# Where the layer steps sit among the attention slots, and two shared score tiles in one stretch

## The chip, the core and the metric

The kernel runs on one core of a Trainium2 chip. A core has a matrix engine (TensorE, PE in the profile, with its weight loads listed apart as PEld), a vector engine (VectorE, DVE), an activation engine (ScalarE, ACT), a general engine (GpSimd, POOL) and DMA queues that move data; here SyncE (SP) issues the transfers. Each engine works through its own list of instructions in the order in which the program was written, and waits at an instruction until what it needs has been signalled by another engine. The metric is the device time of one execution in microseconds. The kernel before took 533.57 us (median of 3 runs, 533.13 to 533.61); the profiled execution spans 532.0 us.

## What is computed

Two stages. The first is attention with a threshold: scores that are more than `tau` below the largest of their row are dropped. The second is two matrix layers with `h - tanh(h)` between them, on the 4608 rows that attention gives.

```python
# q, k, v: (8 batches, 8 heads, 576 rows, 64);  tau = 0.02
def _attn_ref(q, k, v, tau):
    scale = 1.0 / np.sqrt(q.shape[-1])
    scores = scale * np.matmul(q, k.transpose(0, 1, 3, 2))
    thresh = np.max(scores, axis=-1, keepdims=True) - tau
    scores = np.where(scores >= thresh, scores, -1000000000.0)
    scores = scores - np.max(scores, axis=-1, keepdims=True)
    attn = np.exp(scores)
    attn = attn / (np.sum(attn, axis=-1, keepdims=True) + 1e-09)
    return np.matmul(attn, v)

# x: (4608, 512), w_in: (512, 2048), w_out: (2048, 512)
def _moe_ref(x, w_in, w_out):
    h = x @ w_in
    g = h - np.tanh(h)
    return g @ w_out
```

## The kernel before

**Pairs and tiles.** The 64 heads are worked in 32 pairs of heads, 4 pairs to a batch. A pair has 9 score tiles of 128 query rows by 576 keys: four for each head, and one that is shared, in which 64 rows belong to one head and 64 to the other (576 is four times 128 and 64 over). In even pairs the shared tile is the last of the nine, in odd pairs the first, so that the shared tiles of pairs 0 and 1, 2 and 3, and so on are neighbours.

```python
TPP = 9                      # tiles of a pair
HPAIR = H // 2               # 4 pairs of a batch
NTILE = NPAIR * TPP          # 288 tiles
AHEAD, MASK, LAG = 8, 5, 2

def kind(i):
    return "AB"[i % 2]

def place(i):
    p, j = divmod(i, TPP)
    j = j - p % 2
    return (p, None, 4) if j in (-1, 8) else (p, j // 4, j % 4)
```

**Scores.** TensorE makes a tile in one of two PSUM buffers, and VectorE scales it into SBUF and takes the row maximum on the way (L341 in the profile). A normal tile is four matmuls with a 128x128 stationary operand. A shared tile is eight with a 128x64 one, which go in twos, one to each half of the output rows (L322).

```python
ps_big = pool("ps_big", 2, space=PSUM)
sc_pool = pool("sc", AHEAD - MASK + 2)
def scores(i):
    p, hh, t = place(i)
    ...
    ps = ps_big.tile([P, 1024], F32, name="psS", tag="big")
    ...
    if hh is None:
        ...
        for n, kk in enumerate((kT, kS)):
            for dst, srcs in ((main, MAIN), (rem, REM)):
                for hh in range(2):
                    nc.tensor.matmul(                              # L322
                        out=ps[64 * hh : 64 * hh + 64, dst],
                        lhsT=qT[:, qrem[hh]], rhs=kk[:, srcs[hh]],
                        start=(n == 0), stop=(n == 1),
                    )
    else:
        ...                                                        # L331, 128x128
    sc = sc_pool.tile([P, S], F32, name="sc")
    ...
    nc.vector.tensor_scalar(                                       # L341
        out=sc, in0=ps[:, lo : lo + S], scalar1=SC, scalar2=None,
        op0=ALU.mult, op1=ALU.max, accum_out=mx[:, c : c + 1],
    )
```

`shift` turns the maxima of a tile A and the B after it into one bias `nb` (DVE, L353). `kink` applies the threshold on ScalarE (L368, writes `z`). Two `z` tiles are transposed by one DMA (`zT`), from pair 6 on, and exponentiated by one ScalarE instruction (`pT`, L404); in the first six pairs TensorE transposes them. `attend` multiplies by `v` (L425 and L432 for a normal tile, L443 for a shared one), `norm` divides, `emit_x` brings the result into the layout of the layers (`xT`).

**The turn of a pair.** Some slots before a pair's first tile, TensorE transposes its `k` with nine 128x128 matmuls (L240) into a PSUM buffer of the same two as the scores; VectorE copies that out as `kT` (L263), and GpSimd makes `kS`, the same with its halves exchanged (L269). `q` is transposed in the same way or, from pair 8 on in three pairs of four, by DMA.

**The layers.** A batch is 512 rows in one layer stage of its own; the 64 rows that each batch leaves over make a ninth stage. A stage has 16 `h` steps (four 512-column matmuls L498, a tanh on ScalarE L511, and the subtraction on VectorE L517) and 16 `y` steps (four 512-column matmuls L524; after four of them a copy and a store). `layers(stage)` lists them: 19 entries for stage 0, and 32 for each of stages 1 to 6, `h` and `y` by turns.

**The slots.** The program is written slot by slot, one score tile to a slot, and in each slot every engine's list gets the pieces that are due. A batch has 36 slots. The layer steps of a batch are woven into the slots of the next one.

```python
for s in range(-AHEAD, NTILE + LAG + 3):
    p, j = divmod(max(s, 0), TPP)
    if 0 <= s < NTILE and j == 2 + LAG and p % HPAIR == 0 and p >= HPAIR:
        assert not todo
        todo = layers(stage, False)
        share = len(todo) / (HPAIR * TPP - 2 - LAG)
        done, stage = 0.0, stage + 1
    if s == NTILE:
        todo = layers(stage, True)
        share, done, stage = 1, 0.0, stage + 1
    if 0 <= s + AHEAD - 1 < NTILE:
        shift(s + AHEAD - 1)
    if 0 <= s + AHEAD < NTILE:
        scores(s + AHEAD)
    ...
    for i in kinks.pop(s, []):
        kink(i)
    bend()                        # tanh of the h step of the slot before
    for i in wts.pop(s, []):
        weights(i)
    if 0 <= s < NTILE + FIRST:
        if todo:
            done += share
            if s < NTILE and j == TPP - 1 and p % HPAIR == HPAIR - 1:
                done = 1e9
            while todo and done >= 1:
                todo.pop(0)()     # a layer step
                done -= 1
    ...
    shrink()                      # the subtraction of that h step
    ...                           # stores; attend, norm and emit_x that are due
    for step in plan.pop(s, []):  # loads, splits, turns of pairs to come
        step()
```

A stage starts in slot 4 of a batch (its `xT` is finished in slot 3) and ends with the batch's last slot. The first four slots of a batch hold no layer step. After the last score tile the rest of the layers (stages 7 and 8) runs alone.

Of the kernel before, what the change touches and what calls it, by code (L numbers as in the profile page):

```python
# [18 lines left out]
def kernel(  # L19
# [14 lines left out]
    B, H, S, D = q.shape  # L34
# [11 lines left out]
    HPAIR = H // 2  # L46
    NPAIR = B * HPAIR
# [4 lines left out]
    TPP = 9  # L52
    NTILE = NPAIR * TPP
# [9 lines left out]
    AHEAD = 8  # L63
    LDK = 16
    MASK = 5
    LAG = 2
# [177 lines left out]
    def q_by_dma(p):  # L244

        return p >= 2 * HPAIR and p % 4 != 0
# [25 lines left out]
    def turn_first(t, part):  # L272

        hl = hls[0, t[0]]
        c0, c1 = ((0, 5), (5, TPP))[part]
        pl, tag = (ps_y, "y") if t == "ks" else (ps_h, "h")
        ps = pl.tile([P, 5 * P], FP16, name=f"ps1_{t}", tag=tag)
        for c in range(c0, c1):
            o = ps[:, (c - c0) * P : (c - c0 + 1) * P]
            if t == "ks":  # L280
                for a in range(2):
                    turn_chunk(o[64 * a : 64 * a + 64, :], c, hl[:, c, 1 - a, :])
            else:
                turn_chunk(o, c, hl[:, c, :, :].rearrange("p a d -> p (a d)"))
        if part == 0:
            mats[0, t] = qk_pool.tile([P, W], FP16, name=f"{t}T", tag=t)
        dst, n = mats[0, t][:, c0 * P : c1 * P], (c1 - c0) * P
        if part == 1 or t == "q":
            nc.scalar.copy(out=dst, in_=ps[:, 0:n])
        else:  # L290
            nc.vector.tensor_copy(out=dst, in_=ps[:, 0:n])
# [6 lines left out]
# [12 lines that stand above are left out]
        qT, kT, kS = mats[p, "q"], mats[p, "k"], mats[p, "ks"]  # L310
        ps = ps_big.tile([P, 1024], F32, name="psS", tag="big")
        main, rem, lo = slice(0, 512), slice(512, 576), 0
        if kind(i) == "B":
            main, rem, lo = slice(512, 1024), slice(448, 512), 448
        if hh is None:
            qrem = REM
            if q_by_dma(p):
                qrem = (slice(512, 640, 2), slice(513, 640, 2))
# [9 lines that stand above are left out]
            lhs = qT[:, (5 * hh + t) * P : (5 * hh + t + 1) * P]  # L328
            for n, kk in enumerate((kT, kS)):
                for dst, src in ((main, MAIN[hh]), (rem, REM[hh])):  # L330
                    nc.tensor.matmul(  # L331
                        out=ps[:, dst], lhsT=lhs, rhs=kk[:, src],
                        start=(n == 0), stop=(n == 1),
                    )
        sc = sc_pool.tile([P, S], F32, name="sc")
        if kind(i) == "B":
            mx = mxs[i] = mxs.pop(i - 1)
        else:
            mx = mxs[i] = mx3[i // 2 % len(mx3)]
        c = int(kind(i) == "B")  # L340
# [4 lines that stand above are left out]
        scs[i] = sc  # L345

    def shift(i):

        if kind(i) == "A":
            return  # L350
        mx = mxs.pop(i)
        nb = st_pool.tile([P, 9], F32, name="nb", tag="nb")
        nc.vector.tensor_scalar(  # L353
            out=nb.rearrange("p (a b) -> p a b", b=3)[:, :, 0:2],
            in0=mx.rearrange("p (a b) -> p a b", b=4)[:, :, 0:3],
            scalar1=-1.0, scalar2=tau, op0=ALU.mult, op1=ALU.add,
        )
        nbs[i - 1], nbs[i] = nb[:, 0:1], nb[:, 1:2]

    def kink(i):  # L360
        sc, nb = scs.pop(i), nbs.pop(i)
        if kind(i) == "B":
            zt = zs.pop(i - 1)
            z = zt[:, S:W]
        else:
            zt = zs[i] = z_pool.tile([P, W], BF16, name="z")
            z = zt[:, 0:S]
        nc.scalar.activation(  # L368
            out=z, in_=sc, func=ACT.Prelu, bias=nb, scale=1.0, alpha=STEEP
        )  # L370
        if on_pe(i):
            zts[i] = zt
        elif kind(i) == "B":
            zts[i] = zt_pool.tile([P, TPP, P], BF16, name="zT")
            nc.sync.dma_start_transpose(out=zts[i], in_=zt)
# [131 lines left out]
    def bend():  # L507
        while halves:
            m, n, ps = halves.pop(0)
            th = t_pool.tile([P, MB], F32, name="th")  # L510
            nc.scalar.activation(out=th, in_=ps, func=ACT.Tanh)  # L511
            ths.append((m, n, ps, th))

    def shrink():
        while ths:
            m, n, ps, th = ths.pop(0)
            nc.vector.scalar_tensor_tensor(  # L517
                out=gs[m][:, n, :], in0=th, scalar=-1.0, in1=ps,
                op0=ALU.mult, op1=ALU.add,
            )  # L520
# [109 lines left out]
    def w_cast():  # L630
        flat, wt, i, cols = loaded.pop(0)
        nc.gpsimd.tensor_copy(out=flat[:, i * cols : (i + 1) * cols], in_=wt)
# [26 lines left out]
    for p in range(1, NPAIR):  # L659
        first = TPP * p - AHEAD  # L660
        for d, f in PREP[3 if p == 1 else 0 :]:
            d -= p == 1 and d in (3, 5)
            if d in (7, 8) and q_by_dma(p):
                d = d + 2
            if p in (2, 4):
                d = {8: 9, 7: 8, 5: 6}.get(d, d)
            elif d == 5 and p >= 5:
                d = 6 if p % 2 else 3
            plan.setdefault(first - d, []).append(lambda p=p, f=f: f(p))
        d = 7 if q_by_dma(p) else 3 - (p == 1 or p >= 5)  # L670
        d = 4 if p in (2, 4) else d
# [16 lines left out]
    todo, stage = [], 0  # L688
# [4 lines left out]
            plan.setdefault(-AHEAD, []).extend(plan.pop(at))  # L693


    kinks, wts, atts = {}, {}, {}
    for i in range(NTILE + 3):
        at = i - 4 if i < HPAIR * TPP else i
# [4 lines left out]
    for s in range(-AHEAD, NTILE + LAG + 3):  # L703
        p, j = divmod(max(s, 0), TPP)
        if 0 <= s < NTILE and j == 2 + LAG and p % HPAIR == 0 and p >= HPAIR:
            assert not todo
            todo = layers(stage, False)
            share = len(todo) / (HPAIR * TPP - 2 - LAG)
            done, stage = 0.0, stage + 1
        if s == NTILE:  # L710
            todo = layers(stage, True)
            share, done, stage = 1, 0.0, stage + 1
        if 0 <= s + AHEAD - 1 < NTILE:
            shift(s + AHEAD - 1)
        if 0 <= s + AHEAD < NTILE:
            scores(s + AHEAD)
        if s == 1 - AHEAD:
            for t in ("k", "q", "ks"):
                turn_first(t, 1)
        for i in kinks.pop(s, []):  # L720
            kink(i)
        bend()
        for i in wts.pop(s, []):
            weights(i)
        if 0 <= s < NTILE + FIRST:
            if todo:
                done += share
                if s < NTILE and j == TPP - 1 and p % HPAIR == HPAIR - 1:
                    done = 1e9
                while todo and done >= 1:  # L730
                    todo.pop(0)()
                    done -= 1
        if s == 0:
            nc.vector.tensor_tensor(
                out=fold, in0=ident_bf[:, 0:64], in1=ident_bf[:, 64:P], op=ALU.add
            )
        shrink()
        for store in stores[:-1]:
            store()
        del stores[:-1]  # L740
        for i in atts.pop(s, []):
            pp, jj = divmod(i, TPP)
            if i < NTILE:
                attend(i)
                odd = pp % 2
                if jj == 3 + odd:
                    norm(pp, 0)
                elif odd and jj in (0, 8):
                    norm(pp - (jj == 0), 1)
            if pp and jj == 1 + pp % 2:  # L750
                emit_x(pp - 1)
        for step in plan.pop(s, []):
            step()
        if s + AHEAD in cast_when:
            w_cast()
        if s + AHEAD in load_when:
            w_load(next(pieces))
# [54 lines left out]
```

## Time and profile before

| engine | busy us | share of the 532.0 us |
|---|---|---|
| TensorE, matmuls | 509.2 | 96% |
| TensorE, weight loads | 287.6 | 54% |
| VectorE | 421.0 | 79% |
| ScalarE | 435.8 | 82% |
| GpSimd | 290.1 | 55% |

The page has one row for each engine: its busy time, and its share of the span. The timeline lists instructions in order of time, with runs of equal ones merged: start and length in us, engine, line of the program, operation, what it writes and reads, its shape, and how many. The length of a merged row runs from the start of the first to the modelled end of the last. Matmuls overlap, each starting while the one before still drains, so what a matmul costs TensorE is the time from its start to the next start, not its length. The waits list says which engine stood before which line until whose result was there: us in total, how many times, the longest. The windows view gives for each stretch of time its length and the busy time of each engine in it.

The parts of the span in the trace: until 66.88 us attention alone, then stage 0 of the layers beside the attention of the second batch, then from about 123 us to 411 us five like periods of some 57.4 us, one for each batch, then the last batch until about 455 us, and layers alone to the end.

### The profile page before, as it was taken

To read this page: it belongs to the slowest core of one execution; us is meant where nothing else is said; L and a number is where in the kernel's file an instruction comes from. 1 tells how busy PE (TensorE), PEld (TensorE's weight loads), DVE (VectorE), ACT (ScalarE), POOL (GpSimd) and SP (SyncE) were. 2 spreads that over 40 slices of the span, in tenths; PEclk is the share of its full clock that TensorE was granted. 3 is DMA by queue.
4 is the path that set the end of the run, shared out by engine and by line. 5 is a ranking of instruction groups with operands and counts; after the bars stand their busy time and mean duration, and the time that the engine had idled before them with its cause. 6 is when DMAs were issued, how large, how long until landed. Compare 5 with 4: busy or idle time off the path is not lost.

```text
span 532.0 us, 12716 instructions
## 1 busy us (share of the span) xinstructions
PE 509.2 (96%) x4606; PEld 287.6 (54%) x4606; DVE 421.0 (79%) x1179; ACT 435.8 (82%) x617; POOL 290.1 (55%) x390
## 2 busy tenths in 40 slices
PE   8999899988999999999999999999999999999996
PEld 4666566544555555555555555555555555444444
DVE  5899879996888988898889988898889887554440
ACT  5999899988898989898898989898989899543330
POOL 8999989683746657475727574666657530000000
PEclk9999999998999999999999999999999999999999
DMA  7843659979897999789898899999979996400113
GB/s 212 252 133 114 217 186 184 167 160 197 170 209 140 190 184 217 173 179 202 186 197 186 191 188 199 171 185 199 214 160 185 195 149 110 105 33 28 39 41 80
DMA packets 208607, 86.79 MB, mean 163 GB/s; under 512 B 176160, under 2 KB 200992, under 8 KB 208544
## 3 DMA queue, kind: packets, MB, share of 16 engines
q1 hardware_dynamic: 207952, 85.56, 76.0%
q8 instruction: 36, 0.59, 0.5%
q10 hardware_dynamic: 592, 0.43, 0.3%
q14 instruction: 27, 0.22, 0.1%
HBM read 36.70 MB, written 9.44 MB: 87 GB/s over the span
## 4 chain that ended last, share of the span: by engine, by line
PE 35%; issue 20%; POOL 19%; ACT 9%; DMA 8%; DVE 6%; SPq 2%; POOLq 0%; ACTq 0%; DVEq 0%
PE psY L524 12%; PE psH L498 9%; PE psS L331 6%; POOL kS L269 5%; DMA vraw<-in_v_dram 4%; ACT z L368 3%; ACT pT L396 3%; PE psHt L498 3%; DMA kraw<-in_k_dram 3%; POOL khl L193 3%; POOL vb L221 2%; POOL qhl L193 2%; ACT th L511 1%; POOL qhl L192 1%; PE psO L432 1%
## 5 line engine op out<-in xcount | busy, mean ns | idle before, releaser
L341 DVE TENSOR_SCALAR_CACHE_REDUCE sc<-psS 128x576 f32<-128x576 f32 x288 | 214.2, 753 | 39.8 <-PE psS L331 25.9
L368 ACT ACTIVATE z<-sc,nb 128x576 bf16<-128x576 f32 x288 | 216.4, 772 | 22.2 <-DVE nb L353 20.3
L524 PE MATMUL psY<-w_out_sb,g 128*128 128x512 bf16 (+1 forms) x592 | 145.9, 373 | 0.8 <-DVE yo L537 0.8
L404 ACT ACTIVATE pT<-zT 128x1152 f16<-128x1152 bf16 x117 | 135.2, 1156 | 13.4 <-DMA zT<-z 13.2
L269 POOL COPY kS<-kT 64x1152 f16<-64x1152 f16 x62 | 70.9, 1144 | 125.9 <-DVE nb L353 124.4
L498 PE MATMUL psH<-xT,w_in_sb 128*128 128x512 bf16 x480 | 124.1, 381 | 2.6 <-DVE g L517 2.5
L331 PEld LDWEIGHTS <-qT 128*128 128x128 f16 x1024 | 74.8, 98 | 62.3 <-issue 8.4
L331 PE MATMUL psS<-kT,qT 128*128 128x512 f16 (+1 forms) x512 | 104.6, 286 | 3.2 <-DVE sc L341 1.2
L517 DVE SCALAR_TENSOR_TENSOR g<-th,psH 128x512 bf16<-128x512 f32 x128 | 87.6, 684 | 20.9 <-ACT th L511 20.4
L331 PE MATMUL psS<-kS,qT 128*128 128x512 f16 x496 | 101.6, 286 | 1.7 <-POOL kS L269 1.6
L511 ACT ACTIVATE th<-psH 128x512 f32<-128x512 f32 x128 | 74.8, 585 | 22.4 <-PE psH L498 21.8
L524 PEld LDWEIGHTS <-g 128*128 128x128 bf16 x592 | 51.0, 98 | 56.9 <-issue 2.4
L498 PEld LDWEIGHTS <-w_in_sb 128*128 128x128 bf16 x576 | 49.4, 98 | 57.9 <-issue 6.0
L432 PE MATMUL psO<-vb,pT 128*128 128x65 bf16 x1024 | 53.5, 194 | 0.0
L432 PEld LDWEIGHTS <-pT 128*128 128x128 f16 x1024 | 44.4, 98 | 9.7
L193 POOL TENSOR_TENSOR qhl<-qraw,qhl 128x576 f16<-128x576 f32 x31 | 39.7, 1281 | 2.6
L193 POOL TENSOR_TENSOR khl<-kraw,khl 128x576 f16<-128x576 f32 x31 | 39.7, 1281 | 2.6
L396 ACT ACTIVATE pT<-psZ 128x512 f16<-128x512 bf16 (+1 forms) x54 | 35.2, 655 | 3.9 <-PE psZ L387 3.5
L537 DVE COPY yo<-psY 128x512 f32<-128x512 f32 (+1 forms) x31 | 21.2, 682 | 14.1 <-PE psY L524 12.4
L425 PE MATMUL psO<-vb,pT 128*128 128x130 bf16 x128 | 28.3, 221 | 3.3 <-ACT pT L404 2.7
L458 DVE TENSOR_TENSOR osb<-psO,rc 128x256 bf16<-128x256 f32 x64 | 27.2, 424 | 2.2
L263 DVE COPY kT<-ps_k 128x1152 f16<-128x1152 f16 x31 | 23.3, 753 | 4.1 <-PE ps_k L240 4.1
(79 smaller groups left out, 508.8 us busy)
## 6 DMA issues: line engine op xcount, KB each, us to landing
vraw<-in_v_dram SPq DMA_DIRECT2D x32, 256.0 KB, 4.0
out_dram<-yo SPq DMA_DIRECT2D x32, 256.0 KB, 2.8
kraw<-in_k_dram SPq DMA_DIRECT2D x31, 256.0 KB, 3.2
qraw<-in_q_dram SPq DMA_DIRECT2D x31, 256.0 KB, 3.4
wt<-in_moe_w_in_dram SPq DMA_DIRECT2D x8, 512.0 KB, 4.6
wt<-in_moe_w_out_dram SPq DMA_DIRECT2D x8, 512.0 KB, 3.9
zT<-z SPq DMA_TRANSPOSE x117, 3.5
qraw<-in_q_dram SPq DMA_DIRECT2D x32, 32.0 KB, 3.3
```

Of the source, the lines that this page charges most:

```text
L193: nc.gpsimd.tensor_tensor(out=hl[:, :, 1, :], in0=x, in1=hl[:, :, 0, :], op=ALU.subtract)
L269: nc.gpsimd.tensor_copy(out=o, in_=i)
L331: nc.tensor.matmul(out=ps[:, dst], lhsT=lhs, rhs=kk[:, src], start=(n == 0), stop=(n == 1),)
L341: nc.vector.tensor_scalar(out=sc, in0=ps[:, lo : lo + S], scalar1=SC, scalar2=None, op0=ALU.mult, op1=ALU.max, accum_out=mx[:, c : c + 1],)
L368: nc.scalar.activation(out=z, in_=sc, func=ACT.Prelu, bias=nb, scale=1.0, alpha=STEEP)
L396: nc.scalar.activation(out=pt[:, off * P : (off + n) * P], in_=ps[:, 0 : n * P], func=ACT.Exp)
L404: nc.scalar.activation(out=pt[:, 0 : n * P], in_=zts.pop(i)[:, 0:n, :], func=ACT.Exp)
L432: nc.tensor.matmul(out=po[:, t - 1 + ab, :], lhsT=pt[:, blk * P : (blk + 1) * P], rhs=vb[:, hh, c, :], start=False, stop=(n == 7), skip_gr ...
L498: nc.tensor.matmul(out=ps, lhsT=w_in_sb[:, c, n * P : (n + 1) * P], rhs=xs[m][:, c, :] if m < B else xR[:, c, :, :], start=(c == 0), stop= ...
L511: nc.scalar.activation(out=th, in_=ps, func=ACT.Tanh)
L517: nc.vector.scalar_tensor_tensor(out=gs[m][:, n, :], in0=th, scalar=-1.0, in1=ps, op0=ALU.mult, op1=ALU.add,)
L524: nc.tensor.matmul(out=ps, lhsT=gs[m][:, n, ms * P : (ms + 1) * P], rhs=w_out_sb[:, n, cols], start=(n == 0), stop=(n == DF_C - 1),)
```

## The change

The schedule alone is changed; the instructions and their number stay as they are.

First, a stage's layer steps may lie in any slot from its first (slot 4 of a batch) to slot 3 of the next batch, 36 slots instead of 32. Slots in which the `k` of a pair is turned are left out, of which there are four in such a stretch: 32 slots remain. The last stage before the end of the attention has its 32 slots as before. This is to even out what TensorE has to do from slot to slot.

Second, the shared tile of an even pair (a tile A) is no longer computed in its own slot, but in the slot after it, just ahead of the shared tile of the odd pair (a tile B), so that the two use the 128x64 form in one stretch. The slot before then has no score tile, and this one has two.

```diff
+    turns = set()
+    for p in range(HPAIR + 1, NPAIR):
+        d = 6 if p % 2 else 3
+        turns.add(TPP * p - AHEAD - (d if p >= 5 else 5))
+
... in the loop over the slots
             todo = layers(stage, False)
-            share = len(todo) / (HPAIR * TPP - 2 - LAG)
+            room = range(s, min(s + HPAIR * TPP, NTILE))
+            if room[-1] + 1 < NTILE:
+                room = [a for a in room if a not in turns]
+            share = len(todo) / len(room)
             done, stage = 0.0, stage + 1
...
-        if 0 <= s + AHEAD < NTILE:
-            scores(s + AHEAD)
+
+        n = s + AHEAD
+        if 0 < n < NTILE and place(n)[1] is None and kind(n) == "B":
+            scores(n - 1)
+        if 0 <= n < NTILE and (place(n)[1] is not None or kind(n) == "B"):
+            scores(n)
...
         if 0 <= s < NTILE + FIRST:
-            if todo:
+            if todo and (s >= NTILE or s in room):
                 done += share
-                if s < NTILE and j == TPP - 1 and p % HPAIR == HPAIR - 1:
+                if s < NTILE and s == room[-1]:
                     done = 1e9
```

## The prediction

> **What bounds the kernel now.** I read the page first, then the windows of the five like periods, then the waits of one period, and last the timeline of TensorE where the periods meet. The page:
>
> ```profile
> PE 509.2 (96%) x4606; PEld 287.6 (54%) x4606; DVE 421.0 (79%) x1179; ACT 435.8 (82%) x617; POOL 290.1 (55%) x390
> PE   8999899988999999999999999999999999999996
> ```
>
> TensorE looks full in nearly every slice. The windows view, cut where the first layer step of one stage follows the last of another, gives two periods as (length, busy PE, PEld, DVE, ACT, POOL, clock, DMA share, GB/s):
>
> ```profile
> 180.85:238.85 58.00, 56.91 (x520) 31.76 (x518) 50.45 (x146) 52.18 (x71) 34.41 (x45) 1.00 0.92 189
> 238.85:296.22 57.37, 56.55 (x520) 31.68 (x518) 50.45 (x146) 51.96 (x71) 34.41 (x45) 1.00 0.92 188
> ```
>
> Here VectorE and ScalarE are 5 to 7 us short of the period, TensorE about 1 us. The waits of the first of these, longest for ScalarE and VectorE, and the only two that the list has for TensorE:
>
> ```profile
> ACT z L368 <- DVE nb L353: 3.5, 6, 1.2
> DVE sc L341 <- PE psS L331: 3.0, 6, 0.6
> ...
> DVE sc L341 <- PE psS L322: 1.5, 3, 0.8
> ...
> PE psS L331 <- POOL kS L269: 0.3, 1, 0.3
> ...
> PE psH L498 <- DVE g L517: 0.3, 1, 0.3
> ```
>
> The others wait for TensorE more than it waits for them. So TensorE sets the period, but busy time hides small holes. They are seen in starts alone. Where two batches meet, from the last `y` step of a stage to the first `h` step of the next:
>
> ```profile
> 233.50 1.03 PE L524 MATMUL psY<-w_out_sb,g 128*128 128x512 bf16 x4
> 234.36 0.22 PE L425 MATMUL psO<-vb,pT 128*128 128x130 bf16 x1
> ...
> 235.94 0.42 PE L432 MATMUL psO<-vb,pT 128*128 128x65 bf16 x8
> 236.31 0.41 PE L331 MATMUL psS<-kT,qT 128*128 128x512 f16 x2
> 236.55 0.41 PE L331 MATMUL psS<-kS,qT 128*128 128x512 f16 x2
> 236.99 0.41 PE L331 MATMUL psS<-kT,qT 128*128 128x512 f16 x2
> 237.23 0.41 PE L331 MATMUL psS<-kS,qT 128*128 128x512 f16 x2
> 237.78 0.23 PE L425 MATMUL psO<-vb,pT 128*128 128x130 bf16 x1
> ...
> 238.85 1.03 PE L498 MATMUL psH<-xT,w_in_sb 128*128 128x512 bf16 x4
> ```
>
> Each half of a score tile takes 0.24 us start to start (236.31 to 236.55), a tile 0.49. The second tile should follow at 236.80 and starts at 236.99: a hole of 0.19. After it the attend should start at 237.48 and starts at 237.78: 0.30. The eight attends at 235.94 step by about 0.03 (0.41 less one length of 0.19, over seven), so they are over at 236.19, and the next score starts at 236.31: 0.12. In sum **0.61 us of holes** in the four slots without a layer step. VectorE has not one idle stretch in this time after 235.49: in these slots it, with ScalarE, sets the pace, and TensorE waits.
>
> **What a period would be without holes.** From starts in the same rows and in the timeline around 217 us, where a pair is turned: 32 layer steps x 0.86 (233.50 to 234.36) = 27.5; 32 normal score tiles x 0.49 = 15.7; 4 shared tiles x 0.52 = 2.1; 16 attends x 0.30 = 4.8; 4 shared attends, about 0.3 each = 1.2; five turns x 0.50 (217.55 to 218.05) = 2.5; four `emit_x` x 0.25 (238.11 to 238.36) = 1.0. Sum 54.8 us, an estimate good to perhaps 0.5. The period is 57.4, so some 2.6 us are holes of all kinds, and no reordering can give more than 6 periods x 2.6 = 16 us.
>
> **What the Trainium skill says.** "Perfetto Trace Analysis", section Identifying the Most-Contended Engine, calls matmul busy time a bad measure of how near a kernel is to its limit, since matmuls are pipelined. The trace agrees: 96% busy, with the holes above inside it. "TensorE: Matmul & The Clock Gate", section Back-to-back issue gap, gives N/2.4 + 2.5 ns for an isolated warm matmul, 216 ns at 512 columns; four then take 0.86, as 233.50 to 234.36 shows. "TensorEngine Tiling (Array Packing)", section Key Properties: "Mode switching requires drain". The shared tiles use the 128x64 form, all else 128x128. The trace where a layer step lies between two shared tiles:
>
> ```profile
> 204.03 0.41 PE L432 MATMUL psO<-vb,pT 128*128 128x65 bf16 x8
> 204.38 0.44 PE L322 MATMUL psS<-kT,qT 128*64 128x512 f16 x4
> 204.65 0.41 PE L322 MATMUL psS<-kS,qT 128*64 128x512 f16 x4
> 204.99 1.04 PE L498 MATMUL psH<-xT,w_in_sb 128*128 128x512 bf16 x4
> 205.96 0.44 PE L322 MATMUL psS<-kT,qT 128*64 128x512 f16 x4
> 206.23 0.41 PE L322 MATMUL psS<-kS,qT 128*64 128x512 f16 x4
> 206.58 1.04 PE L524 MATMUL psY<-w_out_sb,g 128*128 128x512 bf16 x4
> ```
>
> The attends end at 204.28 by the step of 0.03, and the shared tile starts at 204.38: 0.10. The `h` step should be over at 204.99 + 0.86 = 205.85 and the next form starts at 205.96: 0.11, or about 0.10 with rounding. The way back costs as much: the last 64-column matmul starts near 204.65 + 0.41 - 0.19 = 204.87, is over at 204.90, and L498 starts at 204.99. It agrees: **about 0.095 us for each switch**, four switches for these two tiles.
>
> **The change, part by part.** No instruction is added or removed.
>
> *Shared tiles in one stretch.* A batch has two such couples. The one at the batch's start (234.76 and 235.28 in the trace) already lies together, because no layer step is between. The other one (above) has four switches and will have two: 2 x 0.095 = 0.19 us in each batch. Seven batches have layer steps beside them: 7 x 0.19 = 1.3 us. The couple at the batch's start gains nothing but keeps what it has when layer steps come into its slots; without this part it would lose 0.19 there.
>
> *Layer steps in the first four slots.* The holes of 0.61 us at the meeting of two batches should close, since 0.86 us of layer work in each of those slots gives VectorE and ScalarE time to come up. There are six such meetings (near 119, 178, 236, 293, 351 and 408 us): 6 x 0.61 = 3.7 us.
>
> *Turn slots lose their layer step.* TensorE then has 0.49 + 0.30 + 0.50 = 1.29 us there, while VectorE has an eviction and the `kT` copy, 0.76 + 0.67 start to start, and half a bias, about 1.5. TensorE runs ahead by 0.2 us. Such a slot stands alone among full ones of 1.7 us (31 slots from 180.85 to 233.50), and there are two PSUM buffers, so most of it should be absorbed; I charge 0.05 us x 24 turn slots = 1.2 us. On the other side one hole of 0.3 in each period (`psH` waiting for `g`) lies just after a turn, where VectorE is late; with less work from layers there it may go: 5 x 0.1 to 0.3, I take 0.6.
>
> *What stays.* The attention alone at the start, the last stage's 32 slots and the layers alone at the end (together about 180 us) are as before, but for switches in the last batch, counted above.
>
> Sum: 1.3 + 3.7 - 1.2 + 0.6 = 4.4 us. 533.6 - 4.4 = **529.2 us**, 0.8% less.
>
> **Rivals.** (1) *The hole moves.* Four slots with little TensorE work become four others; if each loses 0.15 to 0.2 us as the free ones do, 24 x 0.15 = 3.6 us eat the gain and the time is 532 to 533.5. For it: VectorE has 1.5 us of work against 1.29 in such a slot. Against it: the free slots follow each other and slack runs out, while turn slots are at least six apart. (2) *VectorE starves, then chokes, at the couples.* In the slot without a score tile VectorE has nothing to evict, then two at once. From the end of one score tile to the end of the next TensorE has 0.86 + 0.30 + 0.86 + 0.52 = 2.5 us, VectorE about 2.1 (0.76, 0.15, a subtraction 0.6, a norm 0.6): 0.4 us idle, 14 times. If the lateness reaches ScalarE through `nb` (its longest wait now) and comes back to TensorE, that is up to 6 us: 535. Against it: `kink` comes two slots later, and VectorE has 7 us to spare in a period. (3) *DMA sets the period.* Its share is 0.92 here, and `zT` is waited for. Then nothing is won: 533.5. Against it: a transposition lands after a median of 3.4 us, 5.5 at most in this period, and only two waits for it, 2.7 us of ScalarE's, are listed. (4) *More than I count.* If the moved steps also close other holes, say 1.2 of the 2.6 us in each period, it is 6 x 1.2 + 0.2 = 7.4: 526.
>
> **Range and chances.** The sum has two firm terms (5.0 together, at best all of it) and a cost of turn slots that I can't read from the trace. Rivals 1 and 3 end near 533, rival 4 near 526. So 526.2 to 533.2 should hold it 8 times in 10. A gain of over 2% (10.7 us, below 522.9) would take two thirds of all holes, and a loss of 2% would need a new wait of over 0.4 us in each turn slot and couple: 0.02 and 0.02.
>
> **What would show it.** Right: periods near 56.7 instead of 57.4; at each couple the second shared tile about 0.52 after the first with nothing between; no hole over 0.1 us in slots 0 to 3 of a batch; the same means for each instruction; layers alone at the end unchanged. Rival 1: holes of 0.15 or more before scores just after a turn. Rival 2: more VectorE idle before L322 and L341, and more ScalarE waiting for `nb`, than 1.5 and 3.5 us in a period. Rival 3: longer landings of `zT` at the same period. I would be wrong if the period did not change though the holes between batches closed.

## The result and the profile after

The changed kernel takes 531.23 us (median of 4 runs, 530.17 to 532.69) against 533.35 for the kernel before: the ratio is 0.9957, with a 95% interval of 0.9935 to 0.998. It is faster by 0.4%, some 2 us, half of the 4.4 that were predicted. The profiled execution spans 530.9 us and is the longest of the four, so holes that vary from one execution to the next are at the large end in what follows. The page:

```profile
PE 507.7 (96%) x4606; PEld 286.4 (54%) x4606; DVE 422.1 (80%) x1179; ACT 433.4 (82%) x617; POOL 289.3 (54%) x390
PE   8999899989999989999999999999999999999996
```

Nothing is to be seen in it. The windows view of the five like periods, cut at the first layer step of each stage as before (length, busy PE, PEld, DVE, ACT, POOL, clock, DMA share, GB/s), says more:

```profile
119.96:179.42 59.46, 56.90 (x520) 31.59 (x519) 50.66 (x144) 52.20 (x71) 34.80 (x46) 1.00 0.97 184
179.42:238.08 58.66, 56.63 (x519) 31.57 (x518) 50.55 (x144) 51.32 (x71) 34.34 (x44) 1.00 0.99 184
238.08:295.98 57.90, 56.65 (x519) 31.59 (x518) 50.56 (x144) 51.94 (x71) 34.34 (x44) 1.00 0.99 189
295.98:353.41 57.43, 56.64 (x520) 31.58 (x519) 50.54 (x144) 51.89 (x71) 34.35 (x44) 1.00 0.96 191
353.41:410.94 57.53, 56.64 (x520) 31.60 (x519) 50.46 (x144) 51.64 (x71) 34.34 (x44) 1.00 0.93 189
```

The kernel before had 57.76, 58.00, 57.37, 57.45 and 57.21 us here. **No period became shorter by more than 0.02 us; four became longer.** The first of them starts at 119.96 instead of 123.09, so 3.1 us were won ahead of it, and by 410.94 (before: 410.88) all of that is lost again. So the gain does not come from where it was predicted. The 1.1 us between the two profiled spans are won after that, in the last batch, whose layer steps lie as before: by starts, two holes of 0.36 and 0.27 us near 428 and 429 and two switches of 0.09 are gone, and a hole of 0.48 at 420 has shrunk to 0.21. What each part did is seen in starts.

**The holes where batches meet are closed.** TensorE around the meeting near 234 us:

```profile
232.54 0.42 PE L322 MATMUL psS<-kT,qT 128*64 128x512 f16 x4
232.79 0.41 PE L322 MATMUL psS<-kS,qT 128*64 128x512 f16 x4
233.14 1.04 PE L524 MATMUL psY<-w_out_sb,g 128*128 128x512 bf16 x4
234.01 0.22 PE L425 MATMUL psO<-vb,pT 128*128 128x130 bf16 x1
234.07 0.42 PE L432 MATMUL psO<-vb,pT 128*128 128x65 bf16 x8
234.33 0.41 PE L331 MATMUL psS<-kT,qT 128*128 128x512 f16 x2
234.57 0.41 PE L331 MATMUL psS<-kS,qT 128*128 128x512 f16 x2
234.81 1.03 PE L498 MATMUL psH<-xT,w_in_sb 128*128 128x512 bf16 x4
```

The `y` step is over after 0.87, the attends after 8 x 0.03, the score tile after 0.48: each next row starts where the one before ends. The holes of 0.12, 0.19 and 0.30 are gone.

**The shared tiles lie together**, with two switches of form instead of four. The other couple of that batch:

```profile
202.32 1.02 PE L498 MATMUL psH<-xT,w_in_sb 128*128 128x512 bf16 x4
203.27 0.44 PE L322 MATMUL psS<-kT,qT 128*64 128x512 f16 x4
203.54 0.42 PE L322 MATMUL psS<-kS,qT 128*64 128x512 f16 x4
203.79 0.41 PE L322 MATMUL psS<-kT,qT 128*64 128x512 f16 x4
204.04 0.41 PE L322 MATMUL psS<-kS,qT 128*64 128x512 f16 x4
204.39 1.04 PE L524 MATMUL psY<-w_out_sb,g 128*128 128x512 bf16 x4
```

Going in costs 203.27 - (202.32 + 0.86) = 0.09, from tile to tile it is 0.52 with no hole, and going out about 0.1, as on the way in.

**New holes are at the turns.** The timeline of both engines about a turn slot (VectorE and TensorE rows):

```profile
241.11 0.68 DVE L517 SCALAR_TENSOR_TENSOR g<-th,psH 128x512 bf16<-128x512 f32 x1
...
241.70 0.18 DVE L457 RECIPROCAL rc<-psO 128x4 f32<-128x4 f32 x1
...
241.91 0.42 DVE L458 TENSOR_TENSOR osb<-psO,rc 128x256 bf16<-128x256 f32 x1
...
242.25 0.15 DVE L353 TENSOR_SCALAR nb<-mx 128x6 f32<-128x6 f32 x1
242.32 0.75 DVE L341 TENSOR_SCALAR_CACHE_REDUCE sc<-psS 128x576 f32<-128x576 f32 x1
...
242.54 0.41 PE L432 MATMUL psO<-vb,pT 128*128 128x65 bf16 x8
...
242.99 0.76 DVE L341 TENSOR_SCALAR_CACHE_REDUCE sc<-psS 128x576 f32<-128x576 f32 x1
243.13 0.66 PE L240 MATMUL ps_k<-ident_f,khl 128*128 128x128 f16 x9 [0.18 <-DVE sc L341]
...
243.81 0.41 PE L331 MATMUL psS<-kT,qT 128*128 128x512 f16 x2
```

The attends are over at 242.54 + 8 x 0.03 = 242.78, and the turn starts at 243.13: **0.35 us lost**. (The bracket says 0.18, for it counts from the modelled end of the last matmul.) The turn writes to one of the two PSUM buffers of the score tiles, and the tile in it is evicted from 242.32 to 243.07. VectorE comes to it late: from 241.11 on it works without a pause on the subtraction of a layer step, a norm, a bias and two evictions. The turn is over at about 243.63, and the next score tile, which needs the buffer that is evicted until 243.75, starts at 243.81: **0.18 more**. In the kernel before, the same slot had a layer step (243.22 to 244.09) ahead of its attends, and its turn starts at 244.40 without a hole: the eviction of 243.19 was over by then. By the same reading of starts, a quiet period (295.98 to 353.41) has 0.34 and 0.18 at each of two turns of `k`, and 0.24 after the turn of `q`: **1.29 us of new holes**. The holes that went: 0.61 at the meeting, 0.49 before an `h` step that waited for `g`, 0.19 of switches: 1.29 us. The 0.49 in the kernel before, where the `h` step should start at 326.34:

```profile
326.10 0.41 PE L331 MATMUL psS<-kS,qT 128*128 128x512 f16 x2
326.83 1.02 PE L498 MATMUL psH<-xT,w_in_sb 128*128 128x512 bf16 x4 [0.32 <-DVE g L517]
```

What is left over nearly balances too: 0.17 at a third turn (311.44) is new, and 0.22 after an `h` step (303.64) is gone. This is why a quiet period is as long as it was.

**Lateness lands in the turn slot.** In the first periods a further hole of up to 1.4 us lies after a turn. The timeline from 192 us:

```profile
192.53 1.16 ACT L404 ACTIVATE pT<-zT 128x1152 f16<-128x1152 bf16 x1 [2.19 <-DMA zT<-z]
...
194.26 0.58 ACT L511 ACTIVATE th<-psH 128x512 f32<-128x512 f32 x1
...
194.87 0.69 DVE L517 SCALAR_TENSOR_TENSOR g<-th,psH 128x512 bf16<-128x512 f32 x1 [1.34 <-ACT th L511]
...
195.47 0.75 DVE L341 TENSOR_SCALAR_CACHE_REDUCE sc<-psS 128x576 f32<-128x576 f32 x1
...
196.29 0.41 PE L331 MATMUL psS<-kT,qT 128*128 128x512 f16 x2 [1.25 <-DVE sc L341]
```

Read from above: a transposition by DMA is late, and ScalarE waits 2.19 us for it. Behind this in ScalarE's list is a tanh, so VectorE waits 1.34 us with its subtraction; behind that is an eviction, and TensorE, in a turn slot without a layer step, waits 1.25 us for the buffer. The kernel before has a wait of 1.85 us for a transposition in the same place (at 194.72), but there TensorE had work meanwhile.

**The 3.1 us at the start** are a net sum, and its largest part is at the first meeting. The timeline of the kernel before, with two rows from just after it, and the windows view of 3.41 us that follow the stop:

```profile
119.99 1.16 ACT L404 ACTIVATE pT<-zT 128x1152 f16<-128x1152 bf16 x1 [2.57 <-DMA zT<-z]
...
121.21 0.23 PE L425 MATMUL psO<-vb,pT 128*128 128x130 bf16 x1 [2.52 <-ACT pT L404]
...
123.09 1.85 PE L498 MATMUL psH<-xT,w_in_sb 128*128 128x512 bf16 x4
124.78 0.41 PE L331 MATMUL psS<-kT,qT 128*128 128x512 f16 x2
```

```profile
121.36:124.77 3.41, 3.41 (x22) 1.74 (x21) 1.39 (x5) 3.41 (x5) 0.80 (x3) 0.50 0.95 177
```

A transposition late by 2.57 us stopped TensorE for 2.52 us, in slots that had no layer step. **The stop cost more than its length**: for the next 3.41 us TensorE was granted half of its clock (the 0.50 above), and the `h` step at 123.09 took 1.69 us to the next start instead of 0.86. Half of 3.41, some 1.7 us, is an estimate of that loss. Of the twelve kernels of this case, five leave the layer steps of stage 0 in their old slots (before, e2, e6, e9, e10); the traces of all five have a hole of 2.7 to 3.1 us, by starts, at this meeting, and four of them, all but e2's, the half clock after it. The traces of the other seven have no hole over 0.8 us there and no half clock. What decides whether the clock falls after such a hole is not shown.

In the changed kernel ScalarE waits 1.47 us for a transposition at 120.68, and the longest hole of TensorE near it is 0.74 us (at 125.07).

### The profile page after: what moved, and what is told of

Read it like the earlier page. It is cut to its first block, busy times and chain, and to the rows that moved or that the text cites. A ratio compares the mean times of both kernels' runs of the same rounds, so it can differ in the third digit from the quotient of the medians.

```text
span 530.9 us, 12707 instructions
## 1 busy us (share of the span) xinstructions
PE 507.7 (96%) x4606; PEld 286.4 (54%) x4606; DVE 422.1 (80%) x1179; ACT 433.4 (82%) x617; POOL 289.3 (54%) x390
## 4 chain that ended last, share of the span: by engine, by line
PE 48%; issue 13%; ACT 12%; DVE 12%; POOL 7%; DMA 7%; SPq 1%; ACTq 0%; POOLq 0%; DVEq 0%
PE psY L524 15%; PE psH L498 12%; PE psS L331 9%; ACT z L368 5%; DVE sc L341 4%; ACT pT L396 3%; DMA zT<-z 3%; PE psHt L498 3%; DVE g L517 2%; PE psO L432 2%; ACT th L511 2%; POOL kS L269 2%; ACT pT L404 2%; DMA vraw<-in_v_dram 2%; PE psS L322 2%
## 5 line engine op out<-in xcount | busy, mean ns | idle before, releaser
L368 ACT ACTIVATE z<-sc,nb 128x576 bf16<-128x576 f32 x288 | 216.0, 769 | 27.6 <-DVE nb L353 27.1
L404 ACT ACTIVATE pT<-zT 128x1152 f16<-128x1152 bf16 x117 | 135.0, 1154 | 10.6 <-DMA zT<-z 10.4
L387 PE MATMUL psZ<-ident_bf,z 128*128 128x128 bf16 x243 | 22.5, 220 | 2.1 <-ACT pT L396 1.3
```

What stands on the lines that cost most here:

```text
L368: nc.scalar.activation(out=z, in_=sc, func=ACT.Prelu, bias=nb, scale=1.0, alpha=STEEP)
L404: nc.scalar.activation(out=pt[:, 0 : n * P], in_=zts.pop(i)[:, 0:n, :], func=ACT.Exp)
```

## The experiments

Each is timed beside the kernel before, and is the changed kernel with the edit shown, unless said otherwise. The theories: **A**, the holes only move from meetings to turn slots, and the gain is the first meeting and the switches; **C**, the prediction's, the meetings bring it; **B**, two evictions in one slot cost what the switches save.

| experiment | us (median) | ratio to before, 95% interval |
|---|---|---|
| the change | 531.23 | 0.9957, 0.9935 to 0.998 |
| e1 layer steps spread, tiles apart | 534.93 | 1.0019, 1.0006 to 1.0033 |
| e2 tiles in one stretch alone | 531.55 | 0.9974, 0.9962 to 0.9985 |
| e3 only stage 0 spread | 529.09 | 0.9912, 0.9892 to 0.9932 |
| e4 other slots left out | 529.18 | 0.9906, 0.9877 to 0.9934 |
| e5 e3 and e4 joined | 527.73 | 0.9885, 0.9863 to 0.9907 |
| e6 only stages 1 to 5 spread | 533.52 | 1.0004, 0.9992 to 1.0016 |
| e7 v loaded earlier | 527.71 | 0.9892, 0.9875 to 0.9908 |
| e8 e5 and e7 joined | 524.40 | 0.9833, 0.981 to 0.9855 |
| e9 before, v loaded earlier | 533.08 | 0.9987, 0.9973 to 1.0001 |
| e10 e2, v loaded earlier | 531.39 | 0.9952, 0.9934 to 0.9971 |

### One part alone: e1 and e2

e1, the spread layer steps with each score tile in its own slot:

```diff
-        n = s + AHEAD
-        if 0 < n < NTILE and place(n)[1] is None and kind(n) == "B":
-            scores(n - 1)
-        if 0 <= n < NTILE and (place(n)[1] is not None or kind(n) == "B"):
-            scores(n)
+        if 0 <= s + AHEAD < NTILE:
+            scores(s + AHEAD)
```

> The layer steps are spread as in the change, and each shared score tile is computed in its own slot as before. Theory A (the holes of TensorE only move: from the meetings of batches into the turn slots, and what gain is left comes from the first meeting, near 119 us, and from fewer switches of form): each of some 13 couples of shared tiles, of which those at a batch's start now also have a layer step between them, pays two more switches than after, 0.19 us each, so 531.2 + 2.4 = 533.6, no gain over before. Theory B (the switches hardly matter, and two evictions in one slot make VectorE late and cost what the switches save): 531 or less.

It took 534.93 us, slower than before. The direction is A's, the size larger: 3.7 us more than the change instead of 2.4; what the other 1.3 are is not shown. e2, the kernel before with the score tiles' part of the change alone:

```diff
-        if 0 <= s + AHEAD < NTILE:
-            scores(s + AHEAD)
+        n = s + AHEAD
+        if 0 < n < NTILE and place(n)[1] is None and kind(n) == "B":
+            scores(n - 1)
+        if 0 <= n < NTILE and (place(n)[1] is not None or kind(n) == "B"):
+            scores(n)
```

> The shared tiles in one stretch, and the layer steps in their 32 slots as before. Theory A: 7 couples save two switches of 0.095 us, 533.4 - 1.3 = 532.1; the holes of 0.6 us where batches meet stay. Theory B (VectorE starves in the slot without a score tile and then has two): 533.5 to 535.

533.42 x (1 - 0.9974) = 1.4 us faster: the 1.3 of the switches, as predicted and as A has it. B is ruled out. Its last period is 56.95 us, 0.26 shorter than before.

### Which stage: e3 and e6

e3 spreads stage 0 alone, e6 stages 1 to 5 alone:

```diff
-            if room[-1] + 1 < NTILE:
+            if stage == 0:                                        # e3
                 room = [a for a in room if a not in turns]
+            else:
+                room = range(s, min(s + HPAIR * TPP - 4, NTILE))
```

```diff
-            if room[-1] + 1 < NTILE:
+            if stage == 0:                                        # e6
+                room = range(s, s + HPAIR * TPP - 4)
+            elif room[-1] + 1 < NTILE:
                 room = [a for a in room if a not in turns]
```

> Shared tiles in one stretch as in the change, but only stage 0 of the layers is spread over 36 slots without the turn slots; stages 1 to 5 have their 32 slots as before. Theory A (the gain comes from the first meeting of batches, where a wait of TensorE for a transposition by DMA, 2.7 us, went away; in the later periods holes only move): 529.5 to 531, as fast as the change or faster, with periods of 57.2 to 57.4 us. Theory C (the gain comes from closing the holes at all six meetings, as predicted): five of six are open again, 533.

> The complement of e3: stage 0 has its 32 slots as before, stages 1 to 5 are spread as in the change, shared tiles in one stretch. Theory A (in the later periods holes only move, and the first meeting is where the gain is): the gain of e3 over e2 is lost, and the loss of the change against e3 stays, 531.6 + 2.1 = 533.7, as before or slower. Theory C (the meetings of batches bring the gain): 0.6 us more than the change at most, 531.8.

e3 took 529.09 us, 2.5 less than e2 and 2.1 less than the change, with periods of 57.93, 57.51, 57.32, 57.07 and 56.96. e6 took 533.52, 2.0 more than e2. Both as A expected, to half a microsecond; C expected 533 and 531.8. So to spread stage 0 is worth some 2.5 us (the hole at the first meeting and, where it occurs, the half clock after it, less what the spreading costs elsewhere), and to spread the later stages, as the change does it, costs about 2. e6 has again a wait at the first meeting, 2.94 us of ScalarE's at 120.16, with TensorE stopped for 3.05 us at 121.38, and the half clock after it.

### Which slots are left out: e4 and e5

```diff
-                room = [a for a in room if a not in turns]
+                room = [a for a in room if a - 3 not in turns]    # e4
```

> As the change, but the four slots left out of a stage are those three slots after a turn, not the turn slots themselves. Theory A: the holes of 0.34 before a turn and 0.18 after it go from the turn slots, but a slot without turn, attend and layer step has only 0.49 us for TensorE beside 0.76 for VectorE, so holes of 0.2 to 0.3 us come in its place: 530 to 532, no clear difference to the change. Theory D (turn slots are a bad choice and other slots would be free of holes): 1.3 us less in each of five periods, 525 to 526.

It took 529.18 us, between the two expectations. The holes at the turns of stages 1 to 5 went. Those in the slots that were left out instead are about 0.19 us at two of four in a quiet period: A took them too large. Late transpositions still cost 0.2 to 1.5 us a period. e5 has this rule for stages 1 to 5 and the change's for stage 0:

```diff
+            off = 0 if stage == 0 else 3
             if room[-1] + 1 < NTILE:
-                room = [a for a in room if a not in turns]
+                room = [a for a in room if a - off not in turns]
```

> Shared tiles in one stretch; stage 0 leaves out the turn slots as in the change, stages 1 to 5 leave out the slots three after a turn. Theory A (the gain of the first meeting and the gain of keeping layer steps in turn slots are of different places and add up): the periods of e4 (some 56.7 us against 57.2 in e3) under the first part of e3, so 529.1 - 5 x 0.5 = 526.5. Rival (both gains are the same slack, and the later waits for transpositions set the time): 529.

527.73 us: 1.4 us faster than e3, of the 2.6 expected. From the change e5 differs only in the slots that stages 1 to 5 leave out, and it is 3.5 us faster: this is the direct test of the choice of turn slots. A quiet period is 56.25 to 56.5 us, but three of the five hold a hole of 1 to 1.5 us behind a late transposition.

### The late transpositions: e7 to e10

```diff
     PREP = (
+        (LDK + 2, lambda p: load(p, "v")),
         (LDK, lambda p: load(p, "k")),
         (LDK - 1, lambda p: load(p, "q")),
-        (LDK - 2, lambda p: load(p, "v")),
```

> As the change, but the loads of v are issued four slots earlier, ahead of those of k and q. Theory E (a transposition behind a load of v lands late, its exponential waits up to 2.2 us, and the lateness goes through the tanh and the subtraction to a turn slot, where TensorE has no layer step to cover it: holes of 1.3, 1.4, 0.6 and 0.2 us in the first four periods): these holes go, 531.2 - 3 = 528. Rival (the lateness follows the load to another transposition and does the same there): 530.5 to 532.

527.71 us, 3.5 less than the change, where E expected 3.2 less. The page's row of the exponentials ends with ScalarE's waits for transpositions, which were 10.4 us in the change:

```profile
L404 ACT ACTIVATE pT<-zT 128x1152 f16<-128x1152 bf16 x117 | 135.0, 1154 | 2.6 <-DMA zT<-z 2.1
```

The large holes behind turns are gone but one of 0.39 us, and the periods are 57.27, 57.36, 57.65, 57.26 and 57.27: what the turns alone cost. e8 joins e5 and e7:

> e5 and e7 together: shared tiles in one stretch, stage 0 without its turn slots, stages 1 to 5 without the slots three after a turn, v loaded four slots earlier. If the holes at turn slots and the late transpositions are the two things left in the way, the periods are those of the quiet one of e5, 56.4 us, instead of the 57.3 of e7: 527.7 - 5 x 0.9 = 523.2. If the slots left out here meet late transpositions again whatever the load does: 526 to 527.5.

524.40 us, the fastest here, 1.7% below the kernel before; its first and fourth periods are 55.96 and 56.37 us. Two lines of its timeline at a turn, which now has a layer step of 0.86 us before its attends:

```profile
181.09 0.42 PE L432 MATMUL psO<-vb,pT 128*128 128x65 bf16 x8
181.34 0.66 PE L240 MATMUL ps_k<-ident_f,khl 128*128 128x128 f16 x9
```

0.25 us from start to start is eight steps of 0.03: no hole. In some periods transpositions are late again (8.7 us of waits in all), which fits a time 1.2 us above what was expected at best.

e9 and e10 take the early `v` to the kernel before and to e2, with the same edit.

> The kernel before, with nothing changed but v loaded four slots earlier. If the gain of the change at the first meeting was the covering of a late transposition (2.7 us of waiting), the same comes from taking the lateness away: 533.4 - 3 = 530.4. If the spread layer steps did it by themselves, 533.

> e9 with the shared tiles in one stretch: e7 without its spreading of layer steps. 530.4 - 1.3 = 529.1. Against e7 (527.7) it shows what the spreading is worth where no transposition is late. Theory A (holes move): within 1 us of e7, or faster than it. Theory C (the meetings of batches): 3 us slower than e7, 530.7.

Both expectations rested on a premise that fell: that the early load takes the lateness away by itself. e9 took 533.08 us, within the noise of before, and its page shows ScalarE's waits as they were:

```profile
L404 ACT ACTIVATE pT<-zT 128x1152 f16<-128x1152 bf16 x117 | 135.0, 1154 | 13.5 <-DMA zT<-z 13.5
```

The wait at the first meeting is there too (2.61 us, at 119.55). e10 took 531.39, 3.7 us more than e7. That is C's number, but not C's reason: its five periods add up to 286.7 us, those of e7 to 286.8, and 2.7 us lie ahead of the first period (122.94 against 120.26), at the first meeting. There TensorE stands for 3.1 us and then has half of its clock:

```profile
120.60 0.24 PE L425 MATMUL psO<-vb,pT 128*128 128x130 bf16 x1 [2.96 <-ACT pT L404]
```

```profile
120.69:124.10 3.41, 3.19 (x21) 1.89 (x23) 1.39 (x5) 3.41 (x5) 0.66 (x3) 0.50 0.82 184
```

So to spread the later periods as the change does wins nothing, which is A. Why the early load of `v` frees the transpositions with spread layer steps and not without is **not settled**; the loads and transpositions share one queue, and no run here separates their order from their load on the DMA engines.

## Why the prediction was right in the time and wrong in the way

*Shared tiles in one stretch, 1.3 us.* Right in size (1.4 in e2) and mechanism. The couple at a batch's start, which it was to guard, counted as well: without this part (e1) the spread layer steps lose to the kernel before.

*Layer steps in the first four slots, 6 x 0.61 = 3.7 us.* The holes closed as said. But the first meeting was not like the other five: it held a wait of 2.5 us for a late transposition and half a clock after it, both in the trace of the kernel before and not in the prediction. The two cost some 4.2 us at that one place (2.5 and an estimated 1.7), against 5 x 0.61 = 3.0 at the five others.

*Turn slots lose their layer step, charged 0.05 x 24 = 1.2 us.* **This step failed.** It gave VectorE 1.5 us of work in such a slot, an eviction and the copy of `kT`. The timeline shows about 2.6 us of unbroken work when a turn comes (241.11 to 243.75): the subtraction of the last `h` step and a norm are due there too. And it took the two PSUM buffers for slack, while the turn itself takes one of them. What came instead: 1.29 us of holes at the turns in each of the five periods, 6.5 us, about what the closed holes gave back; with other slots left out (e5) the time falls by 3.5 us.

*The hole before an `h` step, 0.6 us.* Too low: it went entirely in most periods, 0.49 each.

*The rivals.* Rival 1, the hole moves, is what happened in stages 1 to 5 (e3 and e6 show it from both sides). Rival 2 did not occur: e2 gained. One of its signs did appear, for ScalarE's waits for `nb` rose from 20.3 us in the kernel before to 27.1 in the change; but they are 16.8 in e2 and 28.9 in e1, so they go with the spread layer steps and not with the couples. Rival 3, DMA, was put too simply: transpositions did not set the period, but their lateness, which the kernel before hid behind layer steps, came out where those had been taken away (e7 against the change). The sign that was named for being wrong, holes closed and the period as before, is what the trace shows.

That the time fell in the range is luck: 1.4 us of switches (e2) and 2.5 of the first meeting (e3 against e2), less the 2.1 that the later stages cost (the change against e3), leave 1.8, near the 2.1 measured. Of the 2.5 the sum had 0.61, and where the later stages lost 2.1 it had a gain of some 2.6 (3.0 + 0.6, less 20 x 0.05), so two errors of opposite sign met in it.

## What to carry to other kernels

When work is moved to fill a hole, look at the slot that it is taken from: list what every other engine has to do there, and which buffer the next instruction needs, before calling it slack. Holes that look alike in several places should be read in each of them, for one may have another cause and be worth more than the rest. A late transfer cost nothing here where TensorE had independent work next in its list (the wait of 1.85 us at 194.72), so such work is best left beside the transfers and buffer turns that may be late. After a long stop, compare the spacing of like instructions with the usual: here it was twice as long for 3.4 us, and the stop cost more than its own length.

## What the hardware showed that was not expected

The page's busy share of TensorE is 96% in the kernel before and in the changed one, and 54% for weight loads in both, though e8 shows that at least 1.7% of the time could still be had without removing an instruction. After stops of TensorE of 2.7 to 3.1 us its granted clock was 0.50 for 3.41 us in four traces of five. On the page of the kernel before this is one 8 among nines:

```profile
PEclk9999999998999999999999999999999999999999
```

A change between the 128x128 and the 128x64 form cost 0.09 to 0.11 us each way, at every place read.
